# Attention beside a feed-forward product: DMA transposes for two of four chunks, attention units moved forward, and a last tile in halves

## The chip, the cores and the metric

The kernel runs on one core of a Trainium2 chip. The metric is the device time of one execution in microseconds (us), the median of several runs. The profile is of one execution; its span, from the first to the last instruction, is about 2 us shorter than the measured time (176.4 us beside 178.06 us for the same execution).

The core's engines are named as in the profile: PE (matrix products), PEld (loading of PE's stationary operand), DVE (vector engine), ACT (scalar engine: activation functions), POOL (GpSimd) and SP, which only issues DMAs here. Each engine runs its own instructions in the order of the program; between engines, semaphores say when an operand is ready or a buffer is free.

## The reference

With x of 2048 rows by 448 columns in bf16:

```
xn = layernorm(x)
q, k, v = split(xn @ wqkv)            # 16 heads of 28 columns
logits[s, w] = q[s] . k[s - 2w] / sqrt(28),   w = 0..7   (masked where s - 2w < 0)
s = (softmax(logits) @ v gathered alike) @ wo
y = gelu(xn @ w1 + b1) @ w2 + b2      # 448 -> 1792 -> 448
out = x + s * silu(y)
```

Each row attends to itself and the seven rows 2, 4, ..., 14 before it. The gelu is the tanh form. silu(y) is computed as 0.5 * y * (tanh(y/2) + 1); the factor 0.5 is applied in the last step.

## The kernel before, in words

**Rows.** The even rows come first and then the odd rows, so that a window with a step of 2 becomes a band of 8 neighbouring rows. The 2048 rows are 16 tiles of 128 (t) and 4 chunks of 512 (c). Attention is done in 17 units of 121 queries (b), each with a band of 128 keys.

**Layer norm.** `ln_stats` (DVE) takes mean and variance of a tile, `ln_rstd` (ACT, a logarithm and an exponential) the reciprocal deviation, `ln_apply` (DVE) writes the normalized tile to `xnb[t % 4]`. `ln_tr` transposes it on PE into a PSUM tile `pT` (L172), and `ln_put` copies that into `xnT`, which holds all columns transposed: 128 partitions by 4 slices by rows, with a lead of LEAD columns ahead of row 0.

**Products.** `q_job(c, g)` and `k_job(c, g)` (L185 to L197) make q and k of a chunk for a group g of four heads, four matmuls of 512 columns each, and copy the result to `qT` or `kT`: q on DVE, k on ACT or DVE as the caller says. `v_job(b)` (L199 to L211) makes v for the keys of unit b. `ffn1_even` and `ffn1_odd` make two of the 14 hidden slices of a chunk (k = 0 to 6), and `gelu` (ACT, L239) writes them to `hT`. `ffn2_job(t)` (L257) is the second product of a tile, 14 matmuls; `ffn2_put` (DVE, L264) adds b2 and writes `y_sb`. `silu_job(t)` takes a tanh on ACT (L268) and a product on DVE (L269). `wo_mm` (L288) is the output product, and `wo_put` (L294, L297) multiplies, adds x and issues the store.

**Attention.** `qk_unit(b)` issues 16 small matmuls S = k.q (L312) into two PSUM tiles, two exponentials on ACT (L317) and two multiplications with the band's mask on DVE (L319). `av_unit(b, E)` multiplies with v (L328), spreads the denominators with a shuffle on DVE (L332), and returns `norm`, to be called later: a logarithm and an exponential on ACT (L335, L336), and a product on DVE (L337) that writes `oT`.

**PSUM.** Pool `psA` has two buffers of two banks: for S, and for hidden slices k = 1, 2, 4, 5, 6. Pool `psB` has four buffers of one bank for everything else; they are handed out in turn, and each taker waits until the previous content of its buffer was read.

**Order.** PE, ACT, DVE and POOL follow an order written out by hand (L379 to L485). At the start, eight matmuls on zeros (`busy(8)`), the layer norm of chunk 0 tile by tile, v, q and k of chunk 0, and the first two hidden slices. Then for c = 0, 1, 2 a phase of two parts. The first is `feed_forward_1(c)` (L349 to L376): ACT switches to the table of gelu, PE makes the remaining hidden slices, and in between, at k = 2 and 4, come the transposes of the next chunk's four tiles, the silus of the previous chunk's four tiles and some output products; at its end ACT switches to the table of exp and ln. The second is the attention part: q and k of chunk c + 1 for groups 0 to 2, then four attention units, each followed by one `ffn2_job` and a job "beside" (q and k of group 3, or a v), then a fifth unit with two v jobs, and the first two hidden slices of the next chunk. `ln_apply` for chunk c + 2 is done in this part. After the loop comes the first product of chunk 3 and a tail: units 15 and 16, the four `ffn2_job`s of chunk 3, the silus of its tiles (two of them through exp and ln, `silu_exp_job`, to stay in the same table), and the output products 11 to 15.

SP issues all loads in program order; the x rows of chunk 1 stand behind the first half of w1:

```
    for c0, c1 in ((0, F // 2), (F // 2, F)):
        ...
        if c0 == 0:
            nc.sync.dma_start(x_sb[1][:, :, :], dram_rows(x_par, 4, 4))
```

Of the kernel before, what the change touches and what calls it, by code (L numbers as in the profile page):

```python
# [22 lines left out]
QB = 121  # L23
QW = 122
NB = 17
LEAD = 8
LQ = LEAD + S + 24
SCALE = 1.0 / math.sqrt(DH)
EPS = 1e-5
NG = 12  # L30
# [3 lines left out]
def kernel(  # L34
# [19 lines left out]
    def dram_rows(par, t0, n):  # L54
        cls, r = divmod(t0 * P, S // 2)
        return par[cls, r:r + n * P, :].rearrange("(t p) d -> p t d", p=P)
# [31 lines left out]
    mk_0 = const.tile([P, QW], BF16, name="mk_0")  # L88
    mk_8 = const.tile([P, QW], BF16, name="mk_8")
    wz = const.tile([P, CH], BF16, name="wz")  # L90

    def xt(t):
        return x_sb[t // 4][:, t % 4, :]
# [7 lines left out]
    for dst, c0, c1 in ((wv, 2 * D, 3 * D), (wraw, 0, 2 * D)):  # L101
        nc.sync.dma_start(dst[:, 0:3, 0:c1 - c0], A_wqkv[0:384, c0:c1].rearrange("(k p) f -> p k f", p=P))
        nc.sync.dma_start(dst[:64, 3, 0:c1 - c0], A_wqkv[384:448, c0:c1])
    nc.sync.dma_start(b1t[:], B_b1.rearrange("(m f) -> f m", f=P))
    for c0, c1 in ((0, F // 2), (F // 2, F)):
        nc.sync.dma_start(w1[:, 0:3, c0:c1], B_w1[0:384, c0:c1].rearrange("(k p) f -> p k f", p=P))  # L106
        for r in (0, 64):
            nc.sync.dma_start(w1[r:r + 64, 3, c0:c1], B_w1[384:448, c0:c1])
        if c0 == 0:
            nc.sync.dma_start(x_sb[1][:, :, :], dram_rows(x_par, 4, 4))  # L110
    nc.sync.dma_start(w2[:, :, :], B_w2.rearrange("(m p) c -> p m c", p=P))
    nc.sync.dma_start(b2bc[:], B_b2.rearrange("(o d) -> o d", o=1).to_broadcast((P, D)))
    nc.sync.dma_start(x_sb[2][:, :, :], dram_rows(x_par, 8, 4))
# [8 lines left out]

    nc.gpsimd.memset(vw[:, :, :, 0:1], 1.0)
    nc.gpsimd.memset(vw[:, :, :, DH + 1:32], 0.0)
    nc.vector.memset(wv[64:128, 3, :].bitcast(U32), 0)
    nc.vector.memset(wraw[64:128, 3, 0:2 * D].bitcast(U32), 0)
    nc.vector.memset(wo[:, :, :].bitcast(U32), 0)
# [41 lines left out]
    def ln_tr(t):  # L169
        pT = psB.tile([P, KT, P], BF16, name="pT", tag="B")  # L170
        for kt in range(KT):
            nc.tensor.transpose(pT[:, kt, :], xnb[t % 4][:, kt * P:(kt + 1) * P], ident[:])  # L172
        return pT

    def ln_put(t, pT, copy):
        copy(xnT[:, :, LEAD + t * P:LEAD + (t + 1) * P], pT[:, :, :])


    def qk_weights(which, kt):
# [13 lines left out]
    def q_job(c, g):  # L193
        qk_job(c, g, 0, nc.vector.tensor_copy)

    def k_job(c, g, copy=None):
        qk_job(c, g, 1, copy or nc.scalar.copy)  # L197
# [55 lines left out]
    def ffn2_job(t, put=True):  # L253
# [6 lines left out]
            ffn2_put(t, ps)  # L260
        return ps

    def ffn2_put(t, ps):
        nc.vector.tensor_tensor(out=y_sb[:, t % 4, 0:D], in0=ps[:, :], in1=b2bc[:], op=ALU.add)  # L264

    def silu_job(t):
        th = work.tile([P, D], BF16, name="th", tag="th", bufs=2)
        nc.scalar.activation(th[:], y_sb[:, t % 4, 0:D], ACT.Tanh, scale=0.5)  # L268
        nc.vector.scalar_tensor_tensor(out=g_sb[t % NG][:], in0=th[:], scalar=1.0, in1=y_sb[:, t % 4, 0:D],  # L269
                                       op0=ALU.add, op1=ALU.mult)  # L270
# [18 lines left out]
                             start=(g == 0), stop=(g == 3))  # L289
        return ps  # L290

    def wo_put(t, ps):
        sg = work.tile([P, D], BF16, name="sg", tag="sg", bufs=3)
        nc.vector.scalar_tensor_tensor(out=sg[:], in0=ps[:, :], scalar=0.5, in1=g_sb[t % NG][:],  # L294
                                       op0=ALU.mult, op1=ALU.mult)
        o_t = work.tile([P, D], BF16, name="o_t", tag="o_t", bufs=3)
        nc.vector.tensor_tensor(out=o_t[:], in0=xt(t), in1=sg[:], op=ALU.add)  # L297
        nc.sync.dma_start(dram_rows(out_par, t, 1)[:, 0, :], o_t[:])

    def wo_job(t):  # L300
        wo_put(t, wo_mm(t))
# [47 lines left out]
    def feed_forward_1(c, ps, wos):  # L349

        nc.scalar.preload_act_table_set(SET_GELU)
        nx = 4 * (c + 1)
        gelu(0, ps)
        for k in range(0, MT // 2, 2):
            if k:
                ps = ffn1_even(c, k)
                gelu(k, ps)
            if k + 1 < MT // 2:
                ps = ffn1_odd(c, k + 1)
                gelu(k + 1, ps)  # L360
            if c + 2 < NC and k < 4:
                ln_stats(nx + 4 + k)
                ln_stats(nx + 5 + k)
            if k in (2, 4):
                if c + 1 < NC:
                    for j in (k - 2, k - 1):
                        ln_put(nx + j, ln_tr(nx + j), nc.vector.tensor_copy)
                if c:
                    silu_job(4 * (c - 1) + k - 2)
                    silu_job(4 * (c - 1) + k - 1)  # L370
            for _ in range(2):
                if k >= (2 if c == 3 else 4) and wos:
                    wo_job(wos.pop(0))
        nc.scalar.preload_act_table_set(SET_EXP)
        if c + 2 < NC:
            ln_rstd(nx + 4, 4)  # L376


    with tc.manual_schedule(engines={ENG.PE, ENG.Activation, ENG.DVE, ENG.Pool}):  # L379
        nc.scalar.preload_act_table_set(SET_EXP)  # L380
        busy(8)
        ln_stats(0)
        ln_rstd(0, 1)
        ln_stats(1)
        ln_rstd(1, 1)
        ln_apply(0)
        pT = [ln_tr(0)]
        ln_put(0, pT[0], nc.scalar.copy)
        ln_stats(2)
        ln_rstd(2, 1)  # L390
        ln_apply(1)
        pT.append(ln_tr(1))
        v0 = v_mm(0)
        ln_put(1, pT[1], nc.scalar.copy)
        ln_stats(3)
        ln_rstd(3, 1)
        v_put(0, v0)
        ln_apply(2)
        pT.append(ln_tr(2))
        v1 = v_mm(1)  # L400
        ln_put(2, pT[2], nc.scalar.copy)
        v_put(1, v1)
        ln_apply(3)
        pT.append(ln_tr(3))
        v2 = v_mm(2)
        ln_put(3, pT[3], nc.scalar.copy)
        v_put(2, v2)
        v_job(3)
        for which in range(2):
            for kt in range(KT):  # L410
                qk_weights(which, kt)
        y_sb = work.tile([P, 4, D + 4], F32, name="y", tag="stage", bufs=1)
        late_constants()
        for g in range(4):
            q_job(0, g)
            if g == 3:
                ln_stats(7)
                ln_rstd(4, 4)
            else:
                ln_stats(4 + g)  # L420
            k_job(0, g)
        ps = ffn1_even(0, 0)
        for t in range(4, 8):
            ln_apply(t)

        units = iter(range(NB))
        for c in range(3):
            feed_forward_1(c, ps, [[], [0, 1], [2, 3, 4, 5]][c])
            n = c + 1
            beside = [lambda: q_job(n, 3), lambda: k_job(n, 3), lambda: v_job(4 * n), lambda: v_job(4 * n + 1)]  # L430
            if c == 2:
                beside[1] = lambda: (k_job(3, 3), v_job(12))
                beside[2] = lambda: v_job(13)
                beside[3] = lambda: v_job(14)
            for g in range(3):
                q_job(n, g)
                k_job(n, g, nc.vector.tensor_copy)
            norm = lambda: None
            for i in range(4):
                b = next(units)  # L440
                E = qk_unit(b)
                norm()
                ffn2_job(4 * c + i)
                beside[i]()
                if n + 1 < NC:
                    ln_apply(4 * n + 4 + i)
                norm = av_unit(b, E)
            b = next(units)
            va, vb = 4 * n + 2 + (c == 2), 4 * n + 3 + (c == 2)
            E = qk_unit(b, lambda: v_job(va))  # L450
            v_job(vb)
            norm()
            ps = ffn1_even(n, 0)
            norm = av_unit(b, E)
            norm()
        feed_forward_1(3, ps, [6, 7, 8, 9, 10])
        ffn2_job(12)
        E = qk_unit(15)
        g12 = silu_exp_job(12)
        ffn2_job(13)  # L460
        g12()
        s11 = wo_mm(11)
        norm = av_unit(15, E)
        wo_put(11, s11)
        E = qk_unit(16)
        g13 = silu_exp_job(13)
        norm()
        y14 = ffn2_job(14, False)
        s12 = wo_mm(12)
        norm = av_unit(16, E)  # L470
        g13()
        ffn2_put(14, y14)
        wo_put(12, s12)
        s13 = wo_mm(13)
        norm()
        nc.scalar.preload_act_table_set(SET_GELU)
        wo_put(13, s13)
        silu_job(14)
        y15 = ffn2_job(15, False)
        s14 = wo_mm(14)  # L480
        s15 = wo_mm(15)
        ffn2_put(15, y15)
        wo_put(14, s14)
        silu_job(15)
        wo_put(15, s15)  # L485

# [1 line left out]
_INS = ['A_x', 'A_wqkv', 'A_wo', 'B_x', 'B_w1', 'B_b1', 'B_w2', 'B_b2']  # L488
_OUTS = [((1, 2048, 448), 'bfloat16')]
# [25 lines left out]
```

The softmax here doesn't subtract the row's maximum and nothing guards it: scores larger than these inputs give would overflow.

## Time and profile before

| | |
|---|---|
| time, median of 3 runs | 178.48 us (178.12 to 179.03) |
| span of the profiled execution | 176.4 us |
| granted PE clock | 0.997 |
| PE busy | 163.9 us, 93% of the span |
| ACT busy | 124.7 us, 71% |
| DVE busy | 120.0 us, 68% |
| share of the chain that ended last | PE 68%, ACT 15%, DVE 7%, SP's issuing 4%, DMA 3% |
| largest groups on PE | ffn2 L257 45.1 us, ffn1 L224 40.3 us, q/k L188 29.4 us |
| largest groups on ACT | gelu L239 33.9 us, exp of S L317 32.0 us |

A line of a timeline or a group reads: start and length in us (or busy time and mean in ns), engine, line of the kernel, operation, output <- input with shapes, how often, and in brackets how long the engine had been idle before it and what released it. Matmuls overlap in their pipeline, so the sum of their durations is more than PE's busy time.

### The profile page before, as it was taken

What the parts mean: (1) busy time and instruction counts of PE and PEld (TensorE: products, weight loads), DVE (VectorE), ACT (ScalarE), POOL (GpSimd) and SP (SyncE); (2) the same over time, 40 slices, a digit from 0 to 9 for tenths busy, and PEclk for the clock granted to TensorE, in tenths of its full rate; (3) what the DMA queues carried; (4) which work ended last, traced back from release to release, by engine and by line L of the source; (5) the groups of instructions that cost most, each with busy time, mean ns of one, the idle gap of its engine ahead of it and who ended that gap; (6) DMA issues with size and microseconds to landing.
All of it is one profiled execution on the core that took longest, in us unless ns stands there. A gap on an engine that the chain in (4) does not pass through costs nothing.

```text
span 176.4 us, 3278 instructions
## 1 busy us (share of the span) xinstructions
PE 163.9 (93%) x1324; PEld 75.6 (43%) x1324; DVE 120.0 (68%) x269; ACT 124.7 (71%) x196; POOL 4.5 (3%) x16
## 2 busy tenths in 40 slices
PE   7698999999999989999999989999999999999480
PEld 2343344444454334445454335444555434445140
DVE  6854846667886655977886415987677413978693
ACT  3853397646889699646879699534788699978650
POOL 6030000000000000000000000000000000000000
PEclk9999999999999999999999999999999999999998
DMA  5999972000000000100000000210000000120011
GB/s 145 232 239 320 362 245 50 3 0 4 0 4 0 0 0 4 52 0 4 0 0 6 0 0 0 73 34 0 4 0 0 4 2 0 52 78 30 0 52 52
DMA packets 10991, 9.03 MB, mean 51 GB/s; under 512 B 2593, under 2 KB 10977, under 8 KB 10977
## 3 DMA queue, kind: packets, MB, share of 16 engines
q1 hardware_dynamic: 10688, 8.61, 16.6%
q10 hardware_dynamic: 288, 0.23, 0.4%
q8 instruction: 10, 0.16, 0.4%
q14 instruction: 5, 0.03, 0.1%
HBM read 7.00 MB, written 1.84 MB: 50 GB/s over the span
## 4 chain that ended last, share of the span: by engine, by line
PE 68%; ACT 15%; DVE 7%; SPq 4%; DMA 3%; issue 2%; DVEq 0%
PE ps_y L257 23%; PE ps_h L224 13%; PE ps_qk L188 13%; PE ps_s L288 6%; ACT E L317 4%; PE S L312 3%; PE ps_v L203 3%; DMA x<-in_A_x_dram 3%; PE ps_h L233 3%; ACT hT L239 3%; ACT den L336 2%; PE psO L328 2%; SPq L106 2%; ACT den L335 2%; DVE den L332 2%
## 5 line engine op out<-in xcount | busy, mean ns | idle before, releaser
L317 ACT ACTIVATE E<-S 128x976 bf16<-128x976 f32 x34 | 32.0, 985 | 19.6 <-PE S L312 18.7
L257 PE MATMUL ps_y<-w,hT 128*128 128x448 bf16 x224 | 45.1, 353 | 0.7 <-DVE y L264 0.7
L224 PE MATMUL ps_h<-xnT,w 128*128 128x512 bf16 x168 | 40.3, 380 | 1.5 <-ACT hT L239 1.5
L239 ACT ACTIVATE hT<-ps_h,b1f 128x512 bf16<-128x512 f32 x56 | 33.9, 708 | 2.6 <-PE ps_h L233 2.2
L188 PE MATMUL ps_qk<-xnT,wqk 128*128 128x512 bf16 x128 | 29.4, 379 | 0.6 <-DVE qT L191 0.6
L257 PEld LDWEIGHTS <-hT 128*128 128x128 bf16 x224 | 20.8, 98 | 20.2 <-issue 0.9
L319 DVE TENSOR_TENSOR E<-E,mk_gen 128x976 bf16<-128x976 bf16 x30 | 19.9, 666 | 7.6 <-ACT E L317 7.6
L224 PEld LDWEIGHTS <-w 128*128 128x128 bf16 x168 | 15.4, 98 | 21.4 <-issue 5.7
L337 DVE TENSOR_TENSOR oT<-psO,den 128x484 bf16<-128x484 f32 (+1 forms) x17 | 11.2, 661 | 12.7 <-ACT den L336 12.7
L188 PEld LDWEIGHTS <-wqk 128*128 128x128 bf16 x128 | 12.4, 98 | 15.5 <-issue 1.4
L269 DVE SCALAR_TENSOR_TENSOR g<-th,y 128x448 bf16<-128x448 bf16 x14 | 8.2, 621 | 14.1 <-ACT th L268 14.1
L203 PE MATMUL ps_v<-wv,xnT 128*128 128x448 bf16 x68 | 15.2, 353 | 0.1
L288 PE MATMUL ps_s<-wo,oT 128*128 128x448 bf16 x64 | 13.8, 353 | 1.6 <-DVE oT L337 1.6
L335 ACT ACTIVATE den<-den 128x484 f32<-128x484 f32 (+1 forms) x17 | 10.4, 610 | 5.4 <-DVE den L332 5.4
L191 DVE CAST qT<-ps_qk 128x512 bf16<-128x512 f32 x16 | 10.9, 682 | 3.5 <-PE ps_qk L188 3.5
L156 DVE BATCH_NORM_STATS2 st<-x 128x6 f32<-128x448 bf16 x16 | 9.8, 610 | 5.0 <-DMA x<-in_A_x_dram 5.0
L208 ACT CAST vw<-ps_v 128x448 bf16<-128x448 f32 x17 | 9.1, 536 | 3.9 <-PE ps_v L203 3.8
L332 DVE STREAM_SHUFFLE den<-psO 128x484 f32<-128x484 f32 (+1 forms) x17 | 11.8, 696 | 0.0
L233 PE MATMUL ps_h<-xnT,w 64*128 64x512 bf16 x56 | 10.5, 384 | 0.4
L336 ACT ACTIVATE den<-den 128x484 f32<-128x484 f32 (+1 forms) x17 | 10.3, 605 | 0.5
L264 DVE TENSOR_TENSOR y<-ps_y,b2bc 128x448 f32<-128x448 f32 x16 | 9.9, 618 | 0.9 <-PE ps_y L257 0.8
L294 DVE SCALAR_TENSOR_TENSOR sg<-ps_s,g 128x448 bf16<-128x448 f32 x16 | 9.9, 618 | 0.2
(60 smaller groups left out, 126.5 us busy)
## 6 DMA issues: line engine op xcount, KB each, us to landing
out_dram<-o_t SPq DMA_DIRECT2D x16, 112.0 KB
w<-in_B_w_dram SPq DMA_DIRECT2D x1, 1568.0 KB
w<-in_B_w_dram SPq DMA_DIRECT2D x2, 672.0 KB
x<-in_A_x_dram SPq DMA_DIRECT2D x3, 448.0 KB
wraw<-in_A_wqkv_dram SPq DMA_DIRECT2D x1, 672.0 KB
w<-in_B_w_dram SPq DMA_DIRECT2D x4, 112.0 KB
wo<-in_A_wo_dram SPq DMA_DIRECT2D x16, 24.5 KB
wv<-in_A_wqkv_dram SPq DMA_DIRECT2D x1, 336.0 KB
```

Of the source, the lines that this page charges most:

```text
L188: nc.tensor.matmul(ps[:, :], wqk[:, kt, 16 * which + 4 * g:16 * which + 4 * g + 4, :], xnT[:, kt, LEAD + c * CH:LEAD + (c + 1) * CH], star ...
L203: nc.tensor.matmul(ps[:, :], xnT[:, kt, o:o + P], wv[:, kt, :], start=(kt == 0), stop=(kt == KT - 1))
L224: nc.tensor.matmul(ps[i][:, :], w1[:, kt, m * P:(m + 1) * P], xnT[:, kt, LEAD + c * CH:LEAD + (c + 1) * CH], start=(first and kt == 0), st ...
L233: nc.tensor.matmul(ps[i][:, :], w1[r, 3, m * P:(m + 1) * P], xnT[r, 3, LEAD + c * CH:LEAD + (c + 1) * CH], start=first, stop=not first)
L239: nc.scalar.activation(hT[:, m, :], ps[i][:, :], ACT.Gelu_apprx_tanh, bias=b1f[:, m:m + 1])
L257: nc.tensor.matmul(ps[:, :], hT[:, m, tt * P:(tt + 1) * P], w2[:, m, :], start=(m == 0), stop=(m == MT - 1))
L288: nc.tensor.matmul(ps[:, :], oT[:, g, t * P:(t + 1) * P], wo[:, g, :], start=(g == 0), stop=(g == 3))
L317: nc.scalar.activation(ev, Sp[p2][:, :, :, 0:QW], ACT.Exp, scale=SCALE)
L319: nc.vector.tensor_tensor(out=ev, in0=ev, in1=mkb, op=ALU.mult)
L332: nc.vector.stream_shuffle(den[:, :, 0:n], psO[:, :, 0:n], [0] * 32)
L335: nc.scalar.activation(den[:, :, 0:n], den[:, :, 0:n], ACT.Ln)
L336: nc.scalar.activation(den[:, :, 0:n], den[:, :, 0:n], ACT.Exp, scale=-1.0)
```

## The change

It has six parts.

1. The tiles of chunks 2 and 3 are no longer transposed on PE and copied on DVE: SP issues a transposing DMA from `xnb` straight into `xnT` (`ln_dma`), right after `ln_apply`. Chunk 0 and chunk 1 keep PE's transposes. LEAD grows from 8 to 16, which aligns the destination.
2. q and k of group 0 for chunks 2 and 3 are made inside the first product of the chunk before (at k = 2).
3. The attention part begins with a unit: that unit's S comes before the last four q/k jobs, its AV after them, and then four rounds of unit, `ffn2_job` and v follow. Of the silus in `feed_forward_1`, the second two come at k = 6 instead of 4 (chunks 1 and 2).
4. In the tail, units 15 and 16 come one after the other near the front, only tile 12's silu goes through exp and ln, and tiles 14 and 15 get b2 by one more matmul (a stationary operand of 1/128 times the broadcast b2), so that tanh and product read PSUM.
5. The last tile's second product, silu and output are done in two halves of 224 columns.
6. The x rows of chunk 1 are loaded before b1 and w1, and the start has three more matmuls on zeros.

The core of the diff:

```diff
-LEAD = 8
-LQ = LEAD + S + 24
+LEAD = 16
+LQ = LEAD + S + 16
...
+    nc.sync.dma_start(x_sb[1][:, :, :], dram_rows(x_par, 4, 4))
     nc.sync.dma_start(b1t[:], B_b1.rearrange("(m f) -> f m", f=P))
...
-        if c0 == 0:
-            nc.sync.dma_start(x_sb[1][:, :, :], dram_rows(x_par, 4, 4))
...
+    def ln_dma(t):
+        nc.sync.dma_start_transpose(xnT[:, :, LEAD + t * P:LEAD + (t + 1) * P], xnb[t % 4][:, :])
...
+    def ffn2_biased(pool, tag, t, cs):
...
+        nc.tensor.matmul(ps[:, 0:n], wone[:, :], b2bc[:, cs], start=True, stop=False)
+        for m in range(MT):
+            nc.tensor.matmul(ps[:, 0:n], hT[:, m, tt * P:(tt + 1) * P], w2[:, m, cs],
+                             start=False, stop=(m == MT - 1))
...
+    def silu_psum(t, ps, cs):
...
             if c + 2 < NC and k < 4:
                 ln_stats(nx + 4 + k)
                 ln_stats(nx + 5 + k)
-            if k in (2, 4):
-                if c + 1 < NC:
-                    for j in (k - 2, k - 1):
-                        ln_put(nx + j, ln_tr(nx + j), nc.vector.tensor_copy)
-                if c:
-                    silu_job(4 * (c - 1) + k - 2)
-                    silu_job(4 * (c - 1) + k - 1)
+            if k == 2 and c in (1, 2):
+                q_job(c + 1, 0)
+                k_job(c + 1, 0, nc.vector.tensor_copy)
+            if k in (2, 4) and c == 0:
+                for j in (k - 2, k - 1):
+                    ln_put(nx + j, ln_tr(nx + j), nc.vector.tensor_copy)
+            if c and k in (2, 4 if c == 3 else 6):
+                h = 0 if k == 2 else 2
+                silu_job(4 * (c - 1) + h)
+                silu_job(4 * (c - 1) + h + 1)
...
-        busy(8)
+        busy(9)
...
...
-            for g in range(3):
-                q_job(n, g)
-                k_job(n, g, nc.vector.tensor_copy)
+            qk = [(q_job, g) if w == 0 else (lambda c, g: k_job(c, g, nc.vector.tensor_copy), g)
+                  for g in range(1 if c else 0, 3) for w in range(2)] + [(q_job, 3), (k_job, 3)]
+            for f, g in qk[:-4]:
+                f(n, g)
             norm = lambda: None
-            for i in range(4):
+            vs = iter(range(4 * n, 4 * n + (5 if c == 2 else 4)))
+            for i in range(5):
                 b = next(units)
                 E = qk_unit(b)
                 norm()
-                ffn2_job(4 * c + i)
-                beside[i]()
-                if n + 1 < NC:
-                    ln_apply(4 * n + 4 + i)
+                if i == 0:
+                    for f, g in qk[-4:]:
+                        f(n, g)
+                else:
+                    ffn2_job(4 * c + i - 1)
+                    v_job(next(vs))
+                    if n + 1 < NC:
+                        ln_apply(4 * n + 3 + i)
+                        ln_dma(4 * n + 3 + i)
                 norm = av_unit(b, E)
-            b = next(units)
...
-            E = qk_unit(b, lambda: v_job(va))
-            v_job(vb)
             norm()
+            for b in vs:
+                v_job(b)
             ps = ffn1_even(n, 0)
-            norm = av_unit(b, E)
-            norm()
-        feed_forward_1(3, ps, [6, 7, 8, 9, 10])
+        feed_forward_1(3, ps, [6, 7, 8, 9, 10, 11])
+        E15 = qk_unit(15)
         ffn2_job(12)
-        E = qk_unit(15)
+        E16 = qk_unit(16)
         g12 = silu_exp_job(12)
         ffn2_job(13)
+        n15 = av_unit(15, E15)
+        n16 = av_unit(16, E16)
         g12()
...
+        y14 = ffn2_biased(psB, "B", 14, slice(0, D))
+        n15()
         s12 = wo_mm(12)
...
+        n16()
+        nc.scalar.preload_act_table_set(SET_GELU)
+        s13 = wo_mm(13)
         wo_put(12, s12)
...
+        silu_job(13)
+        silu_psum(14, y14, slice(0, D))
+        halves = (slice(0, D // 2), slice(D // 2, D))
+        y15 = [ffn2_biased(psA, "A", 15, halves[0])]
         wo_put(13, s13)
...
         s14 = wo_mm(14)
...
+        silu_psum(15, y15[0], halves[0])
+        wo_put(14, s14)
+        y15.append(ffn2_biased(psA, "A", 15, halves[1]))
         s15 = wo_mm(15)
...
+        silu_psum(15, y15[1], halves[1])
+        for cs in halves:
+            wo_put(15, s15, cs)
```

## The prediction

> **What bounds the kernel now.** I read three views in this order: busy time by stage, PE's waits, and the timeline at the joints. First, busy time by stage (start:end, length, then busy us and instructions of PE, weight loads, DVE, ACT, POOL; clock; DMA share; GB/s):
>
> ```profile
> 0.00:20.00 20.00, 16.56 (x78) 7.03 (x78) 13.94 (x46) 8.95 (x20) 4.55 (x16) 1.00 0.90 247
> 20.00:58.00 38.00, 38.00 (x345) 17.70 (x345) 26.85 (x65) 28.78 (x44) 0.00 (x0) 1.00 0.18 56
> 58.00:64.00 6.00, 5.11 (x30) 2.19 (x29) 4.55 (x14) 5.21 (x8) 0.00 (x0) 1.00 0.00 0
> 64.00:98.00 34.00, 34.00 (x319) 16.13 (x318) 25.27 (x54) 25.45 (x40) 0.00 (x0) 1.00 0.03 8
> 98.00:104.00 6.00, 5.11 (x30) 2.19 (x29) 1.84 (x4) 5.48 (x9) 0.00 (x0) 1.00 0.00 0
> 104.00:135.20 31.20, 31.20 (x292) 15.01 (x291) 22.37 (x42) 21.39 (x33) 0.00 (x0) 1.00 0.05 16
> 135.20:152.10 16.90, 16.78 (x101) 6.97 (x98) 7.65 (x17) 15.22 (x25) 0.00 (x0) 1.00 0.03 8
> 152.10:176.40 24.30, 17.11 (x146) 8.35 (x144) 17.52 (x36) 14.20 (x20) 0.00 (x0) 0.98 0.13 43
> ```
>
> PE has work without a gap from 20 to 152 us, but for 0.89 us at each of two joints and 0.12 at a third. So any PE work taken out of the middle comes off the span, and so does a gap. The rest of PE's 12.5 idle us is in the front (3.44) and the tail (7.19). Next, PE's waits (us in total, times, longest):
>
> ```profile
> PE ps_s L288 <- DVE oT L337: 1.6, 1, 1.6
> PE ps_h L224 <- ACT hT L239: 1.5, 2, 0.8
> PE pT L172 <- DVE xnb L164: 1.4, 2, 0.8
> PE ps_y L257 <- DVE y L264: 0.7, 1, 0.7
> PE ps_qk L188 <- DVE qT L191: 0.6, 1, 0.6
> ```
>
> The gelu wait is the two joints; oT and y are the tail. The qT wait is the front, and the timeline says what lies behind it: the x rows of chunk 1 land late, and the qT copies stand behind their statistics on DVE.
>
> ```profile
> 15.43 0.63 DVE L156 BATCH_NORM_STATS2 st<-x 128x6 f32<-128x448 bf16 x1 [2.75 <-DMA x<-in_A_x_dram]
> 16.90 1.89 PE L188 MATMUL ps_qk<-xnT,wqk 128*128 128x512 bf16 x8 [0.64 <-DVE qT L191]
> ```
>
> Last, ACT where the feed-forward product hands over to attention (chunk 1); PE ended that product at 70.66 us:
>
> ```profile
> 70.77 1.26 ACT L239 ACTIVATE hT<-ps_h,b1f 128x512 bf16<-128x512 f32 x2 [0.58 <-PE ps_h L233]
> 72.05 1.28 ACT L374 ACT_TABLE_LOAD   x1
> 73.34 0.30 ACT L160 ACTIVATE lnv<-mv,eps_t 128x4 f32<-128x4 f32 x1
> 73.67 0.21 ACT L161 ACTIVATE rstd<-lnv 128x4 f32<-128x4 f32 x1
> 76.38 0.98 ACT L317 ACTIVATE E<-S 128x976 bf16<-128x976 f32 x1 [2.50 <-PE S L312]
> ```
>
> ACT is ready for the first exp at 73.88 and waits 2.50 us: 9.2 us of PE work stand between that product's end and the first AV, which hides the hand-over. The change shortens this cover.
>
> **What the Trainium skill says.** "VectorE: DVE Perf Modes", The three transpose paths: a DMA crossbar transpose of 128x128 bf16 takes 1309 ns; the trace of before has none, so this is my only price. "DMA: Bandwidth & Descriptors", DMA Transpose (X-bar): the SBUF side must be 32-byte aligned; LEAD 16 gives 32 bytes of lead, LEAD 8 gave 16. That is all LEAD is for. "TensorE: Matmul & The Clock Gate", Back-to-back issue gap: N/2.4 + 2.5 ns, so 189 for 448 columns and 96 for 224; the trace agrees nearly (14 ffn2 matmuls in 2.75 us, 196 each). "ScalarE: Activation LUTs", What ACT_TABLE_LOAD costs: 1283 ns plus a drain; the trace has 1283, and the drain is not seen where ACT was idle-free before it (72.03 to 72.05).
>
> **Part by part.**
>
> *Front.* x_1 moves ahead of b1 and w1, so its 0.45 MB land near 11.5 us (an estimate from the bytes ahead of it and the page's 145 and 239 GB/s), before DVE wants them. The 0.64 us wait goes. w1's first half lands 1.4 us later, near 15.4, when PE asks near 18. The extra warm-up matmuls fit gaps of 0.58 and 0.80 us. **-0.6.**
>
> *Transposes.* 32 of 64 PE transposes go. Eight take 0.45 us in the chain, so 4 x 0.45: **-1.8.** The eight DVE copies (415 ns) were hidden. The DMA transposes are issued by SP, which waits for nothing but xnb; nothing but output stores is behind them. The last of a phase's four is ready some 5.4 us after that phase's last S starts; q_job of the next chunk wants it at 10.7 (S 0.33, ffn2 2.75, v 0.76, AV 0.33, four pairs of ffn1 at 1.64). Slack 5.3 us, spacing 4.2 us. One xnb is four 128x128 blocks. Low end: the blocks run together, about 1.3 us plus about 2.8 from the last store's issue to the span's end (173.58 to 176.4): 4.1 us, hidden. High end: blocks in series, 5.2 us a tile: the four fall behind by 3 x 1.0, and the last lands at 5.4 + 3.0 + 5.2 = 13.6, 2.9 us late, in two phases: +5.7. I take the low end, because the 16 DMA engines are all but idle there (share 0.03).
>
> *Phase end.* Five units now stand ahead of, not behind, the four ffn2 jobs, so after the last S PE has ffn2 and one v (3.5 us) where it had two v (1.5 us). ACT after that S: exps to 2.3, v copy, shuffle at 5.0, ln/exp to 6.2, table to 7.5, then two gelus per 1.23 us; PE needs the first freed psA buffer at 12.5 (q and k of group 0 come before it, 1.73 us), freed at 10.0. The joints' gaps go: **-0.89 -0.89 -0.12 = -1.9.**
>
> *First unit of chunks 1 and 2.* Call T the end of that chunk's ffn1. Half of the silus now follow the last gelu on ACT. Chunk 1: gelu to T+1.37, two tanh (1.1, the row of L268) to 2.5, table to 3.8, ln and exp of rstd to 4.35, two E exps to 6.2, mask to 6.9. On DVE the copy of q group 2 is queued behind that mask (0.65): 7.55. AV needs the mask and, as fifth user of the four psB buffers, the buffer of q group 2. PE has only q1, k1, S, q2, k2, q3, k3 = 6 x 0.865 + 0.33 = 5.5. Gap **+2.0**. Chunk 2: no rstd, and two wo products more (1.5) make the cover 7.0; but DVE has two silu products, two output pairs (1.9), q1 and k1 ahead of the mask, so the copy ends at 8.2: **+1.2.** Chunk 0 has no silu and four more q/k jobs ahead: 7.3 of cover against 7.1, nothing. The q/k jobs put into ffn1 are moved, not added.
>
> *Tail*, from the end of ffn1 of chunk 3 (152.1; 24.3 us left). PE's work is now wo10, wo11, S15, ffn2 12, S16, ffn2 13, AV15, AV16, biased 14, wo12, wo13, half 15, wo14, half 15: 1.51+.33+2.75+.33+2.75+.66+2.95+1.52+1.45+.76+1.45 = 16.5, without a wait: ACT's exps of unit 15 free psA at 4.5 for S16 at 4.6, oT of units 15 and 16 is ready at 11.1 and 12.2 (shuffles, ln, exp and product in their order on DVE and ACT), before wo14 at 14.4 wants the first. Then tanh of a half 0.4, product 0.4, and four half output steps, 1.4 in all: o_t at 18.8, as DVE has 15 us of work in it. Plus 2.85 to the end: 21.65. **-2.65.** Three bias matmuls are in this sum, and two y additions are gone. The halves shorten tanh and product, not the last put: 4 short instructions for 2 long.
>
> Sum: -0.6 -1.8 -1.9 +3.2 -2.65 = -3.75. 178.48 - 3.75 = **174.7 us**.
>
> **The rivals.**
> 1. *The hand-over hides* (ACT's chain is shorter or psB is not the limit): no +3.2, 171.5. For it: DVE and ACT are idle a third of the time. Against: the silus stand in program order after gelu 6, and the chain above uses measured durations throughout. Chance 0.12.
> 2. *Late DMA transposes*: PE waits for the transposes at q group 0 in two phases, 174.7 + 5.7 = 180.4, slower than before. For it: the price of one block, and that nothing in the trace shows four at once. Against: idle DMA engines, 5.3 us of slack. Chance 0.12.
> 3. *The tail gives half*: DVE, with 15 of 18.8 us filled, holds up psB buffers, or 15 matmuls of 224 columns are bound by their weight loads (98 ns each, no overlap) and the last stores queue: tail -1, 176.4. For it: the tail of before lost 2.3 us on oT and y. Chance 0.16.
> The forecast has 0.60.
>
> **How the numbers follow.** The likeliest is 174.7. Rival 1 (171.5) and rival 3 (176.4) are inside the range; beyond 176.4 I go to 178.2 for a partly late transpose, half of the 5.7 on top of the forecast being 177.6. Rival 2 in full is left out, with something for both ends. Range 171.2 to 178.2. Faster by over 0.5% means under 177.6: forecast, rival 1 and rival 3 but for a little, 0.84. Within 0.5%: 0.05, the partly late transposes. Slower: 0.11, rival 2.
>
> **What would show it.** In the changed profile: ps_qk no longer waits for qT near 16 us; the waits of ps_h for hT L239 are gone; new PE waits of 2.0 and 1.2 us appear at the first AV (psO) or its psB buffer after ffn1 of chunks 1 and 2, with E, its mask or a qT copy as releaser; 32 pT matmuls are left; from the end of the last ffn1 to the end it is about 21.7 us. Wrong if PE waits for a transposing DMA at ps_qk, if those two gaps are missing, or if PE has gaps between the last products.

## The result, and the profile after

The changed kernel takes 171.2 us (171.11 to 171.52, 4 runs) beside 178.75 us of the kernel before on the same chip: ratio 0.957, interval 0.951 to 0.963. The forecast was 174.7 us in a range of 171.2 to 178.2, so the direction was right and the gain about twice what was forecast. The spans of the two profiled executions are 176.4 and 169.8 us, 6.6 us apart. The medians are 7.5 us apart, because the profiled execution of before (178.06 us) was its quickest and the profiled one of the changed kernel (171.52 us) its slowest. Executions of one kernel differ by up to 4 us, so the ratios and intervals below leave out those more than 1.5% above the quickest of the same kernel, while the medians count all.

Busy time by stage of the changed kernel, with the stages cut where PE goes from one kind of work to another (columns as in the prediction: stage, length, then busy us of PE, weight loads, DVE, ACT, POOL; clock; DMA share; GB/s):

```profile
0.00:17.79 17.79, 16.32 (x74) 7.06 (x76) 13.47 (x46) 8.96 (x20) 4.65 (x17) 1.00 0.80 222
17.79:30.40 12.61, 12.22 (x72) 5.19 (x72) 6.97 (x23) 9.71 (x17) 0.00 (x0) 1.00 0.74 237
...
50.70:69.56 18.86, 18.75 (x128) 7.93 (x123) 13.07 (x30) 14.51 (x23) 0.00 (x0) 1.00 0.09 20
69.56:89.70 20.14, 18.62 (x211) 9.18 (x214) 15.27 (x31) 16.47 (x25) 0.00 (x0) 1.00 0.09 20
89.70:108.48 18.78, 18.67 (x123) 7.86 (x123) 10.18 (x22) 14.43 (x23) 0.00 (x0) 1.00 0.09 21
108.48:129.50 21.02, 20.50 (x231) 10.13 (x230) 16.36 (x31) 16.32 (x23) 0.00 (x0) 1.00 0.06 18
129.50:148.65 19.15, 19.04 (x121) 8.09 (x111) 8.96 (x19) 15.61 (x26) 0.00 (x0) 1.00 0.04 13
148.65:169.80 21.15, 17.24 (x163) 10.00 (x161) 16.30 (x35) 13.15 (x19) 0.00 (x0) 1.00 0.14 45
```

The reader should see three things. A joint is the passage from one chunk's attention part into the next chunk's first product. The stages that hold the joints (50.70, 89.70 and 129.50 us) now have 0.11 us of idle PE each. Idle time has appeared in the stages after them, 1.52 us from 69.56 and 0.52 from 108.48, which had none. And the tail, from the end of the last first product, is 21.15 us long; before it was 24.35.

PE's waits in the changed kernel:

```profile
PE psO L350 <- DVE qT L195: 1.9, 2, 1.5
PE ps_w L369 <- DVE wz L98: 1.3, 1, 1.3
PE ps_qk L192 <- DVE xnT L177: 0.3, 1, 0.3
PE ps_h L228 <- issue: 0.2, 1, 0.2
```

The waits for gelu (hT), oT, xnb, y and the one of a q/k job for qT are gone. That of ps_w, 1.3 us at the start, stood in the kernel before as well, and the 0.3 us for xnT stand ahead of the first q of chunk 1. One line matters: the first AV (the product with v) of chunks 1 and 2, which writes psO, now waits for the copy of a q, 1.5 us in chunk 1 and 0.5 in chunk 2. This is the timeline of it in chunk 1; the first product ended at 69.56 us:

```profile
69.67 1.27 ACT L243 ACTIVATE hT<-ps_h,b1f 128x512 bf16<-128x512 f32 x2 [1.87 <-PE ps_h L237]
70.83 1.04 ACT L290 ACTIVATE th<-y 128x448 bf16<-128x448 f32 x2
71.88 1.28 ACT L400 ACT_TABLE_LOAD   x1
73.62 1.84 ACT L339 ACTIVATE E<-S 128x976 bf16<-128x976 f32 x2
75.49 0.67 DVE L341 TENSOR_TENSOR E<-E,mk_gen 128x976 bf16<-128x976 bf16 x1 [0.20 <-ACT E L339]
76.08 0.68 DVE L195 CAST qT<-ps_qk 128x512 bf16<-128x512 f32 x1
76.81 0.40 PE L350 MATMUL psO<-E,vw 128*32 128x122 bf16 x16 [1.46 <-DVE qT L195]
```

It is the chain that the prediction wrote down, link by link: last gelu, two tanh, table load (the two short instructions for rstd after it are among the lines left out), two exps, mask, q copy, AV.

The transposing DMAs come next: first their line in the changed kernel (minimum, median and maximum of SP's issue time in ns), then its busy time in two stretches after the fourth of them, which SP issues at 55.92 us:

```profile
L180 SPq DMA_TRANSPOSE xnT<-xnb x8: 1189/1190/1307, 43.5 to 94.8; - x8
```

```profile
57.00:58.00 1.00, 1.00 (x6) 0.47 (x5) 0.18 (x1) 0.95 (x3) 0.00 (x0) 1.00 0.64 131
58.00:59.00 1.00, 1.00 (x6) 0.42 (x5) 1.00 (x2) 1.00 (x1) 0.00 (x0) 1.00 0.00 0
```

131 GB/s for 1 us is one tile's 131 KB, and nothing moves after 58 us: the tile is over about 2.1 us after its issue began. PE's q job reads it at 61.38, 3.4 us later.

### The profile page after: what moved, and what is told of

Same layout as the page of the kernel before. It is cut to its first block, busy times and chain, and to the rows that moved or that the text cites. A ratio compares the mean times of both kernels' runs of the same rounds, so it can differ in the third digit from the quotient of the medians.

```text
span 169.8 us, 3258 instructions
## 1 busy us (share of the span) xinstructions
PE 161.6 (95%) x1301; PEld 75.2 (44%) x1312; DVE 116.2 (68%) x262; ACT 124.6 (73%) x195; POOL 4.6 (3%) x17
## 4 chain that ended last, share of the span: by engine, by line
PE 70%; DVE 9%; SPq 8%; DMA 5%; ACT 5%; issue 1%
PE ps_y L261 23%; PE ps_h L228 17%; PE ps_qk L192 6%; PE ps_v L207 6%; PE ps_s L310 6%; DMA x<-in_A_x_dram 5%; SPq L108 4%; PE ps_h L237 3%; PE psO L350 3%; PE ps_yb L274 3%; PE S L334 3%; SPq L112 2%; ACT hT L243 1%; SPq L110 1%; DVE st L157 1%
## 5 line engine op out<-in xcount | busy, mean ns | idle before, releaser
L228 PE MATMUL ps_h<-xnT,w 128*128 128x512 bf16 x161 | 39.8, 380 | 0.5 <-issue 0.2
L261 PE MATMUL ps_y<-w,hT 128*128 128x448 bf16 x196 | 39.5, 353 | 0.0
L261 PEld LDWEIGHTS <-hT 128*128 128x128 bf16 x196 | 18.0, 98 | 16.7
L291 DVE SCALAR_TENSOR_TENSOR g<-th,y 128x448 bf16<-128x448 bf16 x13 | 7.6, 622 | 12.9 <-ACT th L290 12.9
L207 PE MATMUL ps_v<-wv,xnT 128*128 128x448 bf16 x68 | 15.7, 353 | 0.1
L316 DVE SCALAR_TENSOR_TENSOR sg<-ps_s,g 128x448 bf16<-128x448 f32 (+1 forms) x17 | 10.1, 592 | 3.6 <-PE ps_s L310 3.6
L195 ACT CAST kT<-ps_qk 128x512 bf16<-128x512 f32 x7 | 4.1, 582 | 7.1 <-PE ps_qk L192 7.1
L207 PEld LDWEIGHTS <-xnT 128*128 128x128 bf16 x68 | 6.3, 98 | 6.0 <-ACT xnT L177 0.6
```

What stands on the lines that cost most here:

```text
L195: copy((qT, kT)[which][:, g, LEAD + c * CH:LEAD + (c + 1) * CH], ps[:, :])
L207: nc.tensor.matmul(ps[:, :], xnT[:, kt, o:o + P], wv[:, kt, :], start=(kt == 0), stop=(kt == KT - 1))
L228: nc.tensor.matmul(ps[i][:, :], w1[:, kt, m * P:(m + 1) * P], xnT[:, kt, LEAD + c * CH:LEAD + (c + 1) * CH], start=(first and kt == 0), st ...
L261: nc.tensor.matmul(ps[:, :], hT[:, m, tt * P:(tt + 1) * P], w2[:, m, :], start=(m == 0), stop=(m == MT - 1))
```

## The experiments

The first four make one part of the change alone on the kernel before. Their ratios are to the kernel before on the same chip (median 178.41 us, 35 executions). A `...` in a diff marks lines left out.

**DMA transposes alone.**

```diff
+LEAD = 16
...
-                if c + 1 < NC:
+                if c == 0:
                     for j in (k - 2, k - 1):
                         ln_put(nx + j, ln_tr(nx + j), nc.vector.tensor_copy)
...
                     ln_apply(4 * n + 4 + i)
+                    ln_dma(4 * n + 4 + i)
```

> The kernel before with the DMA transposes for chunks 2 and 3 alone (LEAD 16 with them). Theory (the transposes cost PE their own time and nothing else): 32 PE transposes of the chain's 0.056 us each go, -1.8 us, 0.990 of before; the three joints keep their gaps, since the joints are set by ACT and by the normalisation of the fifth unit. Rival (the joints absorb it: PE only waits longer for ACT in the same stage, because ACT, which has 15.5 us of work in the 17.6 us of each of these stages, sets their length): -0.3 us or less, 0.998 to 1.000. Rival of the prediction (the transposes land late): slower.

Measured: 178.37 us, ratio 0.9993 (0.9965 to 1.0021). From the last S of a phase to the end of the next ffn1 it was 17.57 us in both phases and is 17.13: 0.44 saved of the 0.9 that PE no longer works (S is the product k.q of a unit). Two lines of its PE waits:

```profile
PE ps_h L227 <- ACT hT L242: 2.5, 2, 1.2
PE ps_s L291 <- DVE oT L340: 1.6, 1, 1.6
```

The wait for gelu was 1.5 us in two pieces and is 2.5. The theory's 0.990 lies outside the interval; the measured ratio is the rival's. The trace explains it in part only: in the old order the joint takes half of the 1.8 us back. The other 0.9 us, a ratio of 0.995, would lie outside the interval too, and where it went is not shown.

**Units first alone.** This is the attention part's new order: transposes stay on PE, all q/k jobs stay after the first product, and the silus stay at k = 2 and 4.

```diff
+            for f, g in qk[:-4]:
+                f(n, g)
             norm = lambda: None
-            for i in range(4):
+            vs = iter(range(4 * n, 4 * n + (5 if c == 2 else 4)))
+            for i in range(5):
                 b = next(units)
                 E = qk_unit(b)
                 norm()
-                ffn2_job(4 * c + i)
-                beside[i]()
...
+                if i == 0:
+                    for f, g in qk[-4:]:
+                        f(n, g)
+                else:
+                    ffn2_job(4 * c + i - 1)
+                    v_job(next(vs))
...
```

> The kernel before with the attention part's new order alone: all q/k jobs after the first product, four of them before the first unit's S and four after, then four rounds of unit, ffn2 and v; silus stay at k = 2 and 4, transposes on PE. Theory (each joint costs more than the gap counted in PE's idle time, since a wait of 0.5 us for oT lies between two matmuls of one merged group): -(0.89+0.5) twice and -(0.12+0.5), together -3.4 us, and no wait at the first unit, since 7.3 us of q/k work and S cover ACT's hand-over: 0.981 of before. Rival (the prediction's count, the gaps alone): -1.9 us, 0.989.

Measured: 175.06 us, ratio 0.9832 (0.9792 to 0.9871), about -3.0 us; the count of gaps alone (0.989) is outside. In its profile the three stages from the first hidden slice to the end of the first product are 3.7 us shorter together, at the edge of the interval. There is no wait of ps_h for hT and none at the first AV. Where the extra comes from is in a row of the list of groups that the prediction passed over, the weight loads of L233, first before and then with units first (after the bar, the idle time ahead of them and what ended it):

```profile
L233 PEld LDWEIGHTS <-w 64*128 64x128 bf16 x56 | 2.3, 93 | 8.9 <-issue 6.4 <-DVE oT L337 1.8 <-DMA wo<-in_A_wo_dram 0.4
```

```profile
L233 PEld LDWEIGHTS <-w 64*128 64x128 bf16 x56 | 1.7, 94 | 6.8 <-issue 6.4 <-DMA wo<-in_A_wo_dram 0.4
```

The row's 1.8 us of waiting for oT is gone. Before, PE stood three times for 0.6 us at the weight load of a hidden slice, and the profile names as releaser DVE's product for oT, which empties the PSUM buffer of the fifth unit. The timeline of before shows one of the three, in chunk 1:

```profile
60.00 0.67 DVE L337 TENSOR_TENSOR oT<-psO,den 128x484 bf16<-128x484 f32 x1 [1.31 <-ACT den L336]
60.00 1.11 PE L233 MATMUL ps_h<-xnT,w 64*128 64x512 bf16 x4
60.72 0.09 PEld L233 LDWEIGHTS <-w 64*128 64x128 bf16 x1 [0.61 <-DVE oT L337]
```

The fourth weight load comes only when oT is written, and yet the four matmuls count as busy without a break for 1.11 us. The same four with units first:

```profile
60.52 0.61 PE L233 MATMUL ps_h<-xnT,w 64*128 64x512 bf16 x4
```

**Tail alone.**

```diff
-        feed_forward_1(3, ps, [6, 7, 8, 9, 10])
+        feed_forward_1(3, ps, [6, 7, 8, 9, 10, 11])
+        E15 = qk_unit(15)
         ffn2_job(12)
+        E16 = qk_unit(16)
...
+        y14 = ffn2_biased(psB, "B", 14, slice(0, D))
...
```

> The kernel before with the new tail alone (units 15 and 16 together, biased second products, last tile in halves, wo 11 at the end of the first product). Prediction: -2.65 us, 0.985 of before. What the two traces show from the end of the last first product to the end (24.35 against 21.15 us): -3.2 us, 0.982. Rival (part of that is only work moved across the joint): -2 us or less, 0.989.

Measured: 174.97 us, ratio 0.9846 (0.9807 to 0.9886), -2.75 us; its own tail is 21.34 us long (151.96 to 173.3), 3.0 less than before. The interval covers the prediction's 0.985 and the traces' 0.982; the rival's 0.989 lies just outside. What units 15 and 16 together and the biased second products each bring was not separated.

**Front alone.**

```diff
+    nc.sync.dma_start(x_sb[1][:, :, :], dram_rows(x_par, 4, 4))
     nc.sync.dma_start(b1t[:], B_b1.rearrange("(m f) -> f m", f=P))
...
-        if c0 == 0:
-            nc.sync.dma_start(x_sb[1][:, :, :], dram_rows(x_par, 4, 4))
...
-        busy(8)
+        busy(9)
...
+        busy(2)
```

> The kernel before with the front alone (x rows of chunk 1 loaded before b1 and w1, three more matmuls on zeros). Prediction: -0.6 us, 0.9965 of before. By the traces' first ffn1 matmul: -0.83 us, 0.995. Rival (given back within chunk 0, where the x rows of chunk 2 land later than PE wants its transposes copied, or absorbed by the wait for ACT at the first joint): 0 to -0.3 us, 0.998 to 1.000.

Measured: 177.62 us, ratio 0.9993 (0.9962 to 1.0024): nothing that the timing can tell, though the forecast of -0.6 us is just inside the interval. In its profile the qT wait is gone and the first ffn1 matmul starts at 17.69 us instead of 18.62. The other profiles say why one pair of executions decides nothing. With the old front that matmul starts at 17.95, 18.51, 18.62, 19.13 and 19.40 us in five profiles, and in each of them DVE's statistics wait for the load of chunk 1's x rows, until 14.68 us in the earliest and 15.94 in the two latest. With the new front it starts between 17.69 and 18.00 in nine profiles. So the part takes away a spread of 1.45 us: in these profiles it is worth about 0.1 to 1.6 us, by when the rows happened to land.

The next four are the changed kernel again and three changes of it, on one chip.

**The changed kernel again.**

> The changed kernel once more, on the same chip as the next three, as what they are compared with: 171.1 to 171.5 us as before, since its executions kept the full PE clock.

Measured: 171.16 us (171.11 to 171.53).

**Transposes of chunks 2 and 3 back on PE.**

```diff
+            if k in (0, 2) and c in (1, 2):
+                for j in (k, k + 1):
+                    ln_put(nx + j, ln_tr(nx + j), nc.vector.tensor_copy)
             if k == 2 and c in (1, 2):
                 q_job(c + 1, 0)
...
-                        ln_dma(4 * n + 3 + i)
```

> The changed kernel with the transposes of chunks 2 and 3 back on PE (at k = 0 and 2, ahead of the q/k jobs that read them). In the kernel before, taking them away saved only 0.44 us in each of two stages, because PE then waited longer for the gelus. Theory (in the changed kernel PE, not ACT, sets the length of these stages, since two more us of PE work stand ahead of the gelus): the full 0.9 us a stage comes back, +1.8 us on the changed kernel. Rival (ACT still sets part of it, as before): +0.9 us or less.

Measured: 175.16 us, +4.0, more than either expected. The stage from the first hidden slice to the end of ffn1 grew from 14.66 to 16.58 us in chunks 1 and 2, 0.9 of it PE's work and 0.7 a wait:

```profile
PE ps_qk L192 <- ACT hT L243: 1.4, 2, 0.7
```

The q job that follows the transposes waits for a gelu, because the transposes take psB buffers, and the next in turn is one that still holds a hidden slice. Their copies on DVE have to be in xnT, too, before q can start. So with q and k of group 0 inside the first product the DMA transposes are worth 4 us, in the old order nothing that can be timed. That is not their worth in every new order: PE transposes with q and k after the product and the new tail were not run.

**Silus at k = 4.** The second two silus of chunks 1 and 2 go back ahead of the last gelus.

```diff
-            if c and k in (2, 4 if c == 3 else 6):
+            if c and k in (2, 4):
```

> The changed kernel with the second two silus of chunks 1 and 2 at k = 4, as before, not at k = 6 behind the last gelu. Theory (the wait at the first AV, 1.46 us in chunk 1 and 0.46 in chunk 2 with some more inside the q/k jobs, is the chain last gelu, two tanh, table load, exp, mask, q copy): the chain is shorter by the two tanh, 1.04 us, so about -1.0 us in chunk 1 and -0.5 to -0.9 in chunk 2, together -1.5 us on the changed kernel. Rival (ACT has no room at k = 4 and the gelus of k = 5 and 6 come later by as much): no change, 0 to -0.3 us.

Measured: 169.50 us (169.43 to 169.59), -1.66. From the end of the first product's work to the first AV it was 7.25 and 6.44 us in chunks 1 and 2, and is 6.32 and 5.70: 0.93 and 0.74, together 1.67. What is left of the wait:

```profile
PE psO L350 <- DVE qT L195: 0.5, 1, 0.5
```

**q and k of group 0 after the first product.**

```diff
-            if k == 2 and c in (1, 2):
-                q_job(c + 1, 0)
-                k_job(c + 1, 0, nc.vector.tensor_copy)
...
-                  for g in range(1 if c else 0, 3) for w in range(2)] + [(q_job, 3), (k_job, 3)]
+                  for g in range(3) for w in range(2)] + [(q_job, 3), (k_job, 3)]
```

> The changed kernel with q and k of group 0 of chunks 2 and 3 after the first product again, ahead of the attention part's first unit. Theory (the same two jobs, 1.73 us, cover ACT's hand-over there, while inside the first product they cover nothing, as PE no longer waits at the joints): the waits at the first AV go, -1.5 to -1.9 us on the changed kernel. Rival (inside the product they do cover something: without them PE reaches the hidden slices before ACT has freed psA and waits there): what is gained at the first unit is lost in the product, 0 us.

Measured: 169.77 us (169.69 to 170.31), -1.4. No wait at the first AV remains, and none of ps_h for hT has come. The two jobs cover more after the product than in it: that edit of the change cost 1.4 us, given the silus at k = 6, a little less than the theory's 1.5 to 1.9.

The last four, and the kernel before that goes with them (178.30 us, 27 executions), ran on another chip than the changed kernel's 171.16 us; a difference of 0.1 or 0.2 us between the two chips decides nothing.

**Both remedies.** The two edits above together.

> The changed kernel with both remedies for the first unit: silus at k = 4 and q/k of group 0 after the first product. Theory (both shorten the same wait, of which the silus at k = 4 left 0.5 us in chunk 1): 169.0 us, 0.5 below the silus alone. Rival (with both, ACT has the most to do inside the first product and PE the least, so PE waits for gelus there): 169.5 to 170.5 us, with waits of ps_h for hT.

Measured: 169.38 us (169.32 to 169.53), 0.12 below the silus alone, so neither expectation holds in full. No wait of ps_h for hT is on PE's list. The time from the first hidden slice of a chunk to the first AV after it says what became of the 0.5:

| kernel | chunk 1, us | chunk 2, us |
|---|---|---|
| changed kernel | 21.91 | 22.62 |
| silus at k = 4 | 20.99 | 21.89 |
| q and k of group 0 after the product | 20.58 | 22.54 |
| both | 20.58 | 22.13 |

In chunk 1 both together gain 0.41 us on the silus alone; in chunk 2 they lose 0.24. PE's list has no wait for that loss, and its cause stays open.

**The q copy between the masks.** With the silus at k = 4:

```diff
-                E = qk_unit(b)
+                if i == 0:
+                    E = qk_unit(b, lambda: qk[-4][0](n, qk[-4][1]))
+                else:
+                    E = qk_unit(b)
                 norm()
                 if i == 0:
-                    for f, g in qk[-4:]:
+                    for f, g in qk[-3:]:
```

> The changed kernel with the silus at k = 4 and the copy of q of group 2 put between the two masks of the first unit on DVE. Theory (the first AV waits for the buffer of q group 2, whose copy of 0.6 us stands behind the second mask): the wait of 0.5 us left in chunk 1 becomes 0.1 or nothing, 169.1 us. Rival (AV waits for the second mask itself, which now comes later by the copy): 169.5 us or up to 0.3 more.

Measured: 169.24 us (169.08 to 169.74), ratio 0.9483 (0.9448 to 0.9519) to the kernel before. The wait of psO has gone from PE's list, and the first AV of chunk 1 begins 5.71 us after the product instead of 6.32. But it now lasts 0.70 us instead of 0.40: the second mask, whose half of E it reads too, ends only at 75.13 us, 0.26 after the AV began. So the rival is partly right, and half of the gain is lost again. It has the lowest median of all versions, 1.9 us below the changed kernel, most of it from the silus; its executions (169.08 to 169.74) overlap with those of both remedies.

**Tile 15 whole.**

```diff
-        y15 = [ffn2_biased(psA, "A", 15, halves[0])]
+        y15 = ffn2_biased(psA, "A", 15, slice(0, D))
         wo_put(13, s13)
         s14 = wo_mm(14)
...
-        for cs in halves:
-            wo_put(15, s15, cs)
+        wo_put(15, s15)
```

> The changed kernel with tile 15 whole in the tail (one biased second product of 448 columns, one tanh, one product, one output put) instead of in halves. Theory (a half shortens the last tanh and product by 0.4 us and the last store by 0.3, and costs two short DVE steps): +0.3 to +0.6 us on the changed kernel's 171.2. Rival (the halves are the core of the tail's gain): +1.5 us or more. Rival (the extra steps eat it): 0.

Measured: 171.72 us (171.57 to 172.15), +0.56, as the theory has it; in the profile the tail is 21.69 us long instead of 21.15. The halves are a sixth of what the tail brought.

**Gaps of before filled.** Nine matmuls on zeros in the tail of the kernel before:

```diff
         norm = av_unit(16, E)
+        warm(6)
...
         silu_job(14)
+        warm(3)
         y15 = ffn2_job(15, False)
```

> The kernel before with nine matmuls on zeros in its tail, in the two stretches where PE waits: six after the output product of tile 12 (wait of 1.6 us for oT) and three ahead of the second product of tile 15 (0.7 us). Theory (a part of what the change brought is not in the profile of before: in some of its executions the granted clock falls to 0.988 and the last product runs at half speed after these gaps, which puts 1.5 to 2 us on the execution): the best time stays within 0.3 us of before's 177.2, the executions near 180 go, and the median falls by 0.4 to 0.8 us. Rival (the spread comes from the loads at the start, whose landing differs between executions): the same spread, 177.2 to 180.3, and the same median, plus up to 0.5 us for the matmuls added.

Measured: 178.12 us (177.23 to 181.17, 22 runs) beside 178.30 of before (177.19 to 180.32, 27 runs), ratio 0.9993 (0.9970 to 1.0016). Of the executions before, 4 took over 180 us, with a granted clock of 0.988; with the gaps filled 1 of 22 did. That points to the theory, but so few executions can differ by chance, and the median moved by only 0.2 us, so it explains little of the result.

## Why the prediction was off

Term by term, the prediction beside what the profiles show. The middle figures for the phase end come from the kernel with units first:

| term of the sum | predicted, us | measured, us | from |
|---|---|---|---|
| front | -0.6 | -0.5 | first q/k of chunk 1 at 30.93, now 30.47 |
| PE transposes | -1.8 | -1.8 | ffn1 stage 13.84 and 13.83 with units first, in the changed kernel 14.66 with 1.73 of q/k in it, so 12.93 |
| phase end | -1.9 | -3.7 | see below |
| first unit | +3.2 | +2.65 | 7.25 and 6.44 less 5.52 of work |
| tail | -2.65 | -3.2 | 24.35, now 21.15 |
| sum | -3.75 | -6.55 | spans: -6.6 |

Of the 3.8 us by which the medians went beyond the forecast, 2.8 are in these terms; 1.0 lies in which executions were profiled.

**The step that failed is the phase end**, "The joints' gaps go: -0.89 -0.89 -0.12 = -1.9". The cause was right, and all three joints closed; the size was wrong. From the first hidden slice to the end of ffn1, less the 0.33 us of AV inside, it was 15.39 us for chunks 1 and 2 and 15.05 for chunk 3. With units first it is 13.84, 13.83 and 14.44: 1.55, 1.56 and 0.61 saved. The prediction read PE's idle time and the list of PE's waits, where a stretch counts as busy once a matmul stands at the array, even if the next weights wait for a buffer. The missing 0.5 to 0.66 us a joint stood under the weight loads: three waits of 0.6 for oT, 1.8 us in all.

**First unit of chunks 1 and 2**: place, releaser and chain were as forecast, and the silus at k = 4 removed what the chain says they should. It was sized 0.55 too long: each link was set after the end of the one ahead, but ACT's overlap a little (two tanh end 2.31 us after the product, not 2.5; the AV comes at 7.25, not 7.55), and in chunk 2 the AV comes at 7.9 instead of 8.2, both counted from the end of ffn1. The 5.52 us of work are the prediction's own figure; where no wait is left, the same six jobs and S take 5.70 (chunk 2 with the silus at k = 4), so about 0.4 of the 2.65 us is not waiting.

**Tail**: PE's work from 148.65 to the last half of tile 15 took 16.5 us as forecast, without a wait. The rest came out shorter: the last o_t ended 18.6 us after the start instead of 18.8, and the span ended 2.55 us after it with the half-size store, where 2.85 was taken over from the whole store.

**Front and transposes** came out as sized, the front partly by luck: the old front's start differs by 1.45 us between profiles, and the profiled execution of before lay in the middle. The transposes count in full only because the joints closed: alone, they lost half to the wait for ACT. So the prediction's "any PE work taken out of the middle comes off the span" does not hold for a stage that ends in a wait, and its terms are not independent. Alone, the four parts come to 0.1, 3.0, 2.75 and 0.1 us, about 6; all together, with the silus at k = 4 and one q copy moved, to 9.1 us.

**The rivals**: the measured time is close to the 171.5 us of rival 1, but by luck, since its reason does not hold: the hand-over does not hide. Late transposes did not happen: the fourth tile was over about 2.1 us after its issue began, and PE read it 5.5 us after. The tail did not give half.

## What to carry to other kernels

Before pricing a gap on the matrix engine, read what its weight loads waited for as well as its own idle time: in this profile waits for an output buffer stood there while a matmul counted as busy. Taking work from the engine that is busiest overall pays only in stages where it also sets the length; close the wait that ends such a stage first, and the same edit is worth its full size. Where the cover over a hand-over is shortened, move what can go ahead of the chain's first link, here two silus, before anything else.

## What the runs showed of the hardware

A DMA transpose of 128x512 bf16 from SBUF to SBUF holds SP for 1.19 us and was over about 2.1 us after its issue began, though the Trainium skill ("VectorE: DVE Perf Modes", The three transpose paths) has 1309 ns for a 128x128 block alone: four blocks were over in far less than four times that, 5.2 us.

In the profiled execution of the kernel with units first, the second product of tile 15 ran at half speed after PE had waited 1.62 and 0.70 us in the tail:

```profile
162.70 0.93 PE L288 MATMUL ps_s<-wo,oT 128*128 128x448 bf16 x4 [1.62 <-DVE oT L337]
164.32 4.49 PE L257 MATMUL ps_y<-w,hT 128*128 128x448 bf16 x14 [0.70 <-DVE y L264]
```

```profile
165.00:167.00 2.00, 2.00 (x7) 0.73 (x5) 1.97 (x5) 1.34 (x2) 0.00 (x0) 0.50 0.17 57
```

The granted clock there is 0.50, and the 14 matmuls take 4.3 us to the next group instead of 2.65. The stages taken from this profile above end before it. The waits alone do not decide it: in the profiled execution of before, the same two waits of 1.62 and 0.69 us were followed by 14 matmuls in 2.64 us. The new tail has no such waits, and no execution with it showed a mean clock below 0.994; that the waits are the cause is not shown.
